# One block's softmax sums in a single round, its values in existing matmul bursts, and one shared PSUM pool

## Chip, cores, metric

One core of a Trainium2 chip. The metric is device time in microseconds (us) of one execution. A ratio is the mean time of one kernel's runs over that of the other's runs of the same rounds, so not quite the ratio of the medians quoted.

## What the kernel computes

```python
def _attn_ref(q, k, v, E, F):                    # 8 batches, 8 heads, 1024 tokens, head size 64
    k_proj = np.einsum('ks,bhsd->bhkd', E, k)    # 1024 tokens -> 64
    v_proj = np.einsum('ks,bhsd->bhkd', F, v)
    scores = (1 / np.sqrt(64)) * np.matmul(q, k_proj.transpose(0, 1, 3, 2))
    ...                                          # softmax over the 64
    return np.matmul(attn, v_proj)

def _moe_ref(x, w_in, w_out):                    # x: 8192 x 512, from the attention
    h = x @ w_in                                 # 512 -> 2048
    return (h / (1 + np.exp(-1.702 * h))) @ w_out
```

The kernel handles 16 blocks of 512 tokens. Block j's two layers of large matmuls run while the attention of later blocks is threaded between them.

## The kernel before

`eight` is one round of eight small matmuls in eight tiles of the array (64 rows by 32 columns each); the large matmuls use the whole array. A round into another mode, and the way back, is called a burst here. A bank is one buffer of a PSUM pool; a chunk is the matmuls between two slots of the schedule (four in layer 1); u = 0 and 1 are the two halves of a block's heads; landing is the time from a load's issue to its arrival.

```python
ps_f = ...tile_pool(name="ps_f", bufs=4, space=PSUM)      # large matmuls, scores, projections
ps_d = ...tile_pool(name="ps_d", bufs=2, space=PSUM)      # sums
ps_n = ...tile_pool(name="ps_n", bufs=2, space=PSUM)      # values

def sums(h):                                              # blocks 5 to 15
    def go():
        d_ps = [ps_d.tile([P, TB], F32, name="d_ps") for _ in range(2)]
        ...                                               # one round: 8 sums on 32 rows each
        for e in range(2):
            nc.vector.reciprocal(rden[:, e, :], d_ps[e])
        rdr = dram.tile([HP, 2, TB], F32, name="rdr")
        nc.sync.dma_start(out=rdr, in_=rden[0:P:32])
        rbc[h] = att.tile([P, HP, TB], F32, name="rbc")
        for e, r in enumerate((LO, HI)):                  # copied to all rows by DMA
            nc.sync.dma_start(out=rbc[h][r], in_=rdr[None, :, e, :].to_broadcast([D, HP, TB]))
    return go

def norm(h, u):                                           # blocks 3 and 4, u = 0 and 1
    def go():
        d_ps = ...; eight(d_ps, [ones, ones], e)          # sums on all rows
        n_ps = ...; eight(n_ps, [values ...], e)
        for i in range(2):
            nc.vector.reciprocal(rd, d_ps[i])
            nc.vector.tensor_tensor(x_of(h)[:, 2 * u + i, :], n_ps[i], rd, op=ALU.mult)
    return go

def values(h, u): ...                                     # one round, then n_ps[i] * rbc[h]
...
# at(block, slot): slots 0 to 15 follow the chunks of layer 1, O = 16 and on those of layer 2
at(2, 1, norm(3, 0))
at(1, O + 7, proj(2), kv_out(2))
at(2, 11, norm(3, 1))
at(2, O + 6, proj(3), kv_out(3), norm(4, 0))
at(2, O, q_dma(3))
at(3, 9, norm(4, 1))
```

The softmax here doesn't subtract the row's maximum and nothing guards it: scores larger than these inputs give would overflow.

## Time and profile before

| | before |
|---|---|
| median of the first three runs | 514.3 us (514.02 to 514.62) |
| span of the profiled execution | 512.6 us |
| TensorE busy | 505.9 us, 3098 matmuls |
| VectorE busy | 171.7 us |
| granted clock | full in every slice |

TensorE hardly pauses, so where time goes is read from the starts of its groups: the distance from one start to the next, less what the same matmuls take undisturbed. The lines are in the prediction.

### The profile page before, as it was taken

The numbers are of one execution on the slowest core, as the hardware profiler recorded it, in microseconds if no ns is written. First come the engines' busy times: TensorE is split into PE (matmuls) and PEld (weight loads), VectorE is DVE, ScalarE is ACT, GpSimd is POOL, SyncE is SP. The second block draws the span as 40 slices with busy tenths as digits, with TensorE's granted clock in tenths as the row PEclk, the third lists the DMA queues.
The fourth block names the chain that finished last, engine by engine and source line by source line (L and its number), as shares of the span: only waits on it lengthen the run. The fifth ranks groups of instructions, "written<-read, shape, count | busy, mean of one in ns | idle before, by whom it ended". The sixth has DMA issues, their size and how long they took to land.

```text
span 512.6 us, 7250 instructions
## 1 busy us (share of the span) xinstructions
PE 505.9 (99%) x3098; PEld 231.8 (45%) x3098; DVE 171.7 (33%) x222; ACT 264.8 (52%) x444; POOL 78.0 (15%) x97
## 2 busy tenths in 40 slices
PE   8999999999999999999999999999999999999997
PEld 4584444434444444444444444444444444444444
DVE  4523114764861622316251241615214161611000
ACT  1675564554637456372755627374463737244351
POOL 7442051513300051000510024000000000000000
PEclk9999999999999999999999999999999999999999
DMA  9999999999989089650997349990602205050102
GB/s 164 197 203 207 211 141 167 217 169 131 208 125 217 1 177 199 131 160 28 219 169 179 73 89 217 114 245 1 170 1 69 97 4 162 1 166 1 82 1 82
DMA packets 124200, 66.58 MB, mean 130 GB/s; under 512 B 92252, under 2 KB 116060, under 8 KB 122248
## 3 DMA queue, kind: packets, MB, share of 16 engines
q0 software_dynamic: 84400, 29.37, 51.1%
q1 hardware_dynamic: 39688, 36.49, 28.2%
q8 instruction: 24, 0.39, 0.3%
q10 hardware_dynamic: 80, 0.26, 0.2%
q14 instruction: 8, 0.07, 0.0%
HBM read 70.78 MB, written 16.96 MB: 171 GB/s over the span
## 4 chain that ended last, share of the span: by engine, by line
PE 82%; DMA 13%; issue 3%; POOL 1%; DVE 0%; ACT 0%; POOLq 0%
PE f_ps L369 38%; PE f_ps L401 38%; DMA v_sb<-in_v_dram 9%; DMA w_in_sb<-in_moe_w_in_dram 2%; PE f_ps L166 2%; DMA k_sb<-in_k_dram 2%; PE f_ps L263 2%; PE n_ps L263 1%; PE d_ps L298 0%; POOL k_sb L58 0%; PE f_ps L393 0%; POOL q_sb L64 0%; PE d_ps L263 0%; POOL q_sb L58 0%; POOL v_sb L58 0%
## 5 line engine op out<-in xcount | busy, mean ns | idle before, releaser
L401 PE MATMUL f_ps<-w_out_sb,gT 128*128 128x512 bf16 x1008 | 227.4, 379 | 0.0
L369 PE MATMUL f_ps<-xT,w_in_sb 128*128 128x512 bf16 (+1 forms) x1088 | 226.5, 367 | 0.3 <-DMA w_in_sb<-in_moe_w_in_dram 0.2
L372 ACT ACTIVATE gT<-f_ps 128x512 bf16<-128x512 f32 (+1 forms) x270 | 152.1, 573 | 64.3 <-PE f_ps L369 63.2
L369 PEld LDWEIGHTS <-w_in_sb 128*128 128x128 bf16 x1088 | 105.0, 98 | 116.9 <-issue 2.1
L401 PEld LDWEIGHTS <-gT 128*128 128x128 bf16 x1008 | 95.6, 98 | 120.1 <-issue 11.3
L404 ACT COPY o_sb<-f_ps 128x512 f32<-128x512 f32 x63 | 36.9, 586 | 130.8 <-PE f_ps L401 121.0
L328 DVE TENSOR_TENSOR xT<-n_ps,rbc 128x512 bf16<-128x512 f32 x44 | 28.4, 686 | 203.3 <-PE n_ps L263 122.9
L301 DVE RECIPROCAL rden<-d_ps 128x512 f32<-128x512 f32 x22 | 72.2, 3321 | 0.0
L64 POOL DMA_DIRECT2D q_sb<-in_q_dram x56 | 49.1, 901 | 55.8 <-DMA k_sb<-in_k_dram 42.8
L279 ACT ACTIVATE expT<-f_ps 128x512 bf16<-128x512 f32 (+1 forms) x68 | 35.1, 571 | 27.9 <-PE f_ps L263 27.8
L58 POOL DMA_DIRECT2D k_sb<-in_k_dram x10 | 8.4, 845 | 172.9 <-PE f_ps L166 156.0
L318 DVE RECIPROCAL rdn<-d_ps 128x512 f32<-128x512 f32 x8 | 26.8, 3353 | 3.2 <-PE d_ps L263 3.2
L220 DVE CAST k_b<-f_ps 64x512 bf16<-64x512 f32 x7 | 4.8, 683 | 47.1 <-PE f_ps L166 47.1
L279 ACT ACT_TABLE_LOAD x13 | 16.7, 1283 | 4.7 <-PE f_ps L263 4.5
L283 ACT ACT_TABLE_LOAD x14 | 18.0, 1283 | 0.2
L166 PE MATMUL f_ps<-v_sb,eft 128*64 128x512 bf16 x56 | 13.4, 381 | 0.3 <-DMA v_sb<-in_v_dram 0.3
L166 PE MATMUL f_ps<-k_sb,eft 128*64 128x512 bf16 x56 | 13.6, 382 | 0.0
L395 DVE COPY o_sb<-f_ps 128x256 f32<-128x256 f32 x1 | 0.4, 425 | 38.6 <-issue 38.6
L136 PE MATMUL n_ps<-zeros 128*128 128x512 bf16 x34 | 11.5, 463 | 1.2 <-DVE zeros L107 1.2
L263 PE MATMUL f_ps<-qT,kt 64*32 64x512 bf16 x240 | 12.3, 386 | 0.0
L263 PE MATMUL n_ps<-expT,vq 64*32 64x512 bf16 x208 | 10.4, 377 | 0.0
L263 PEld LDWEIGHTS <-kt 64*32 64x32 bf16 x272 | 3.9, 88 | 13.7 <-issue 13.5
(71 smaller groups left out, 131.6 us busy)
## 6 DMA issues: line engine op xcount, KB each, us to landing
out_dram<-o_sb SPq DMA_DIRECT2D x15, 1024.0 KB
rbc<-rdr SPq DMA_DIRECT2D x22, 512.0 KB
k_sb<-in_k_dram POOLq DMA_DIRECT2D x7, 1024.0 KB, 13.8
v_sb<-in_v_dram POOLq DMA_DIRECT2D x7, 1024.0 KB, 10.4
q_sb<-in_q_dram POOLq DMA_DIRECT2D x56, 128.0 KB, 13.8
w_in_sb<-in_moe_w_in_dram POOLq DMA_DIRECT2D x8, 256.0 KB, 12.2
w_out_sb<-in_moe_w_out_dram POOLq DMA_DIRECT2D x4, 512.0 KB, 14.7
out_dram<-o_sb SPq DMA_DIRECT2D x3, 256.0 KB
```

The costliest lines, as they stand in the source:

```text
L64: nc.gpsimd.dma_start(out=qt[b][:, j], in_=qv[:, j])
L166: nc.tensor.matmul(kvps[b][r], eft(j, slice(e * KP, (e + 1) * KP)), (kt, vt)[e][b][:, :, j, :], start=(j == 0), stop=(j == J - 1))
L263: nc.tensor.matmul(outs[i][r.start + c:r.start + c + 32], lhsTs[i][ri, c:c + 32], rhss[i][ri], start=True, stop=True)
L279: nc.scalar.activation(expT[h][:, 2 * u + i, ts], s_ps[i], AF.Exp, scale=scale)
L283: nc.scalar.preload_act_table(AF.Gelu_apprx_sigmoid)
L301: nc.vector.reciprocal(rden[:, e, :], d_ps[e])
L318: nc.vector.reciprocal(rd, d_ps[i])
L328: nc.vector.tensor_tensor(x_of(h)[:, 2 * u + i, :], n_ps[i], rbc[h][:, 2 * u + i, :], op=ALU.mult)
L369: nc.tensor.matmul(h_ps, w_in_sb[:, kc, fc * P:(fc + 1) * P], xT[j][:, kc, ts], start=(kc == 0), stop=(kc == KC - 1))
L372: nc.scalar.activation(gts[j][:, fc, ts], h_ps, AF.Gelu_apprx_sigmoid)
L401: nc.tensor.matmul(o_ps[n], gts[j][:, fc, n * P:(n + 1) * P], w_out_sb[:, fc, :], start=(fc == 0), stop=(fc == FC - 1))
L404: nc.scalar.copy(osb[j][:, n, :], o_ps.pop(n))
```

## The change

Block 4 is to be treated as blocks 5 to 15 are: one round of sums, two reciprocals in place of four, copies by DMA, and the values in bursts that exist already. The one pool lets sums and values take any of four banks. Two edits come with it: the projection of batch 2 moves one chunk later, and the start is reordered. (The preload of ScalarE's GELU table in block 2 also moves two slots later, behind the moved scores.)

```diff
-    ps_d = ctx.enter_context(tc.tile_pool(name="ps_d", bufs=2, space=PSUM))
-    ps_n = ctx.enter_context(tc.tile_pool(name="ps_n", bufs=2, space=PSUM))
+    ps_x = ctx.enter_context(tc.tile_pool(name="ps_x", bufs=4, space=PSUM))
...                               (sums split into sums and spread, which holds the DMAs)
     tok(0, 3, 0)()
-    q_tr0(1, 0, AC)
-    q_tr0(1, 1, DV)
     x_tr(0, 3, 0)()
-    scores(0, 0, 1)()
+    q_tr0(1, 0, DV)
+    q_tr0(1, 1, DV)
...
-    at(0, 0, scores(0, 1, 1))
-    at(0, 1, gelu_table)
+    at(0, 0, scores(0, 0, 1))
+    at(0, 1, scores(0, 1, 1), gelu_table)
...
-        at(2, O + 3 + 2 * u, scores(5, u))
...
-    at(1, O + 7, proj(2), kv_out(2))
+    at(2, 0, proj(2), kv_out(2))
-    at(2, O + 6, proj(3), kv_out(3), norm(4, 0))
-    at(3, 9, norm(4, 1))
+    at(2, O + 4, scores(5, 0))
+    at(2, O + 6, proj(3), kv_out(3), scores(5, 1), sums(4), spread(4))
...
-            at(j, O, sums(j + 2))
+            at(j, O, sums(j + 2), spread(j + 2))
+        if j == 3:
+            at(j, O, values(4, 0))
+            at(j, O + 6, values(4, 1))
```

More of the change, by code (lines that the diff above doesn't have):

```diff
@@ L133, in warm @@
     def warm(n):
-        w_ps = ps_n.tile([P, TB], F32, name="n_ps")
+        w_ps = ps_x.tile([P, TB], F32, name="x_ps")
         for _ in range(n):
@@ L156, in eft @@
         return efts[j // (J // 2)][:, j % (J // 2), cols]
-    kvps, kbs, qT, expT, xT, rbc = {}, {}, {}, {}, {}, {}
+    kvps, kbs, qT, expT, xT, rbc, rdens = {}, {}, {}, {}, {}, {}, {}
     def proj(b):
@@ L293, in go @@
         def go():
-            d_ps = [ps_d.tile([P, TB], F32, name="d_ps") for _ in range(2)]
+            d_ps = [ps_x.tile([P, TB], F32, name="x_ps") for _ in range(2)]
             for p in range(HP):
@@ L301, in go, with spread @@
                 nc.vector.reciprocal(rden[:, e, :], d_ps[e])
+            rdens[h] = rden
+        return go
+    def spread(h):
+        def go():
             rdr = dram.tile([HP, 2, TB], F32, name="rdr")
-            nc.sync.dma_start(out=rdr, in_=rden[0:P:32])
+            nc.sync.dma_start(out=rdr, in_=rdens.pop(h)[0:P:32])
             rbc[h] = att.tile([P, HP, TB], F32, name="rbc")
@@ L311, in go @@
             e = [expT[h][:, 2 * u + i, :] for i in range(2)]
-            d_ps = [ps_d.tile([P, TB], F32, name="d_ps") for _ in range(2)]
+            d_ps = [ps_x.tile([P, TB], F32, name="x_ps") for _ in range(2)]
             eight(d_ps, [ones, ones], e)
-            n_ps = [ps_n.tile([P, TB], F32, name="n_ps") for _ in range(2)]
+            n_ps = [ps_x.tile([P, TB], F32, name="x_ps") for _ in range(2)]
             eight(n_ps, [vqs[h // NB2 % 2][:, 2 * u + i, :] for i in range(2)], e)
@@ L323, in go @@
         def go():
-            n_ps = [ps_n.tile([P, TB], F32, name="n_ps") for _ in range(2)]
+            n_ps = [ps_x.tile([P, TB], F32, name="x_ps") for _ in range(2)]
             eight(n_ps, [vqs[h // NB2 % 2][:, 2 * u + i, :] for i in range(2)],
@@ L336, in go @@
         def go():
-            d_ps = f_tile([P, 4, D + 1]) if (h, half) == (0, 0) and p > 1 else                 ps_d.tile([P, 4, D + 1], F32, name="d_ps")
+            d_ps = f_tile([P, 4, D + 1]) if (h, half) == (0, 0) and p > 1 else                 ps_x.tile([P, 4, D + 1], F32, name="x_ps")
             for i in range(2):
@@ L352, in go @@
             x_sb = xs.pop((h, p, half)).rearrange("s (i t) d -> s i (t d)", i=2)
-            n_ps = ps_n.tile([P, 2, P], BF16, name="n_ps")
+            n_ps = ps_x.tile([P, 2, P], BF16, name="x_ps")
             for i in range(2):
@@ L439 @@
     tok(0, 3, 0)()
-    q_tr0(1, 0, AC)
+    x_tr(0, 3, 0)()
+    q_tr0(1, 0, DV)
     q_tr0(1, 1, DV)
-    x_tr(0, 3, 0)()
-    scores(0, 0, 1)()
     order = [(half, fc) for fcs in (range(12), range(12, FC)) for half in range(2) for fc in fcs]
-    at(0, 0, scores(0, 1, 1))
-    at(0, 1, gelu_table)
+    at(0, 0, scores(0, 0, 1))
+    at(0, 1, scores(0, 1, 1), gelu_table)
     for p in range(HP):
@@ L470 @@
         at(1, O + 3 + p, x_tr(2, p, 0), x_tr(2, p, 1))
-    for j in (1, 2):
-        at(j, O + 5, gelu_table)
+    at(1, O + 5, gelu_table)
     at(1, O + 4, q_dma(2))
+    at(2, 0, proj(2), kv_out(2))
     at(2, 1, norm(3, 0))
-    at(1, O + 7, proj(2), kv_out(2))
     at(2, 11, norm(3, 1))
-    at(2, O + 6, proj(3), kv_out(3), norm(4, 0))
     at(2, O, q_dma(3))
-    at(3, 9, norm(4, 1))
+    at(2, O + 4, scores(5, 0))
+    at(2, O + 6, proj(3), kv_out(3), scores(5, 1), sums(4), spread(4))
+    at(2, O + 7, gelu_table)
     for b in range(4, B):
@@ L490 @@
         if j + 2 < NBLK:
-            at(j, O, sums(j + 2))
+            at(j, O, sums(j + 2), spread(j + 2))
+        if j == 3:
+            at(j, O, values(4, 0))
+            at(j, O + 6, values(4, 1))
+        if j + 2 < NBLK:
             at(j, O + 6, values(j + 2, 0))
```

## The prediction

> **What bounds the kernel now.** I read the page first: TensorE against the other engines, and the chain that ended last.
>
> ```profile
> PE 505.9 (99%) x3098; PEld 231.8 (45%) x3098; DVE 171.7 (33%) x222; ACT 264.8 (52%) x444; POOL 78.0 (15%) x97
> ...
> PEclk9999999999999999999999999999999999999999
> ...
> PE 82%; DMA 13%; issue 3%; POOL 1%; DVE 0%; ACT 0%; POOLq 0%
> ```
>
> TensorE is 99% busy and the granted clock is full throughout. VectorE at 33% is far from a bound, so time saved there counts only where TensorE waits for it. Busy alone does not say that nothing can be saved: matmuls overlap, so I went on to TensorE's timeline and read differences of start times. These are four stretches of it (start, length, then the group):
>
> ```profile
> 115.08 3.63 PE L401 MATMUL f_ps<-w_out_sb,gT 128*128 128x512 bf16 x16
> 118.64 0.41 PE L263 MATMUL f_ps<-qT,kt 64*32 64x512 bf16 x8
> 118.98 1.90 PE L401 MATMUL f_ps<-w_out_sb,gT 128*128 128x512 bf16 x8
> ...
> 124.95 8.80 PE L369 MATMUL f_ps<-xT,w_in_sb 128*128 128x512 bf16 x40
> 133.68 0.41 PE L263 MATMUL d_ps<-expT,ones 64*32 64x512 bf16 x8
> 133.90 0.40 PE L263 MATMUL n_ps<-expT,vq 64*32 64x512 bf16 x8
> 134.24 5.35 PE L369 MATMUL f_ps<-xT,w_in_sb 128*128 128x512 bf16 x24
> ...
> 141.47 0.54 PE L298 MATMUL d_ps<-expT,ones 64*32 64x512 bf16 x8
> 141.94 10.53 PE L401 MATMUL f_ps<-w_out_sb,gT 128*128 128x512 bf16 x48
> ...
> 154.70 13.98 PE L369 MATMUL f_ps<-xT,w_in_sb 128*128 128x512 bf16 x64
> 168.51 1.89 PE L401 MATMUL f_ps<-w_out_sb,gT 128*128 128x512 bf16 x8
> 170.33 0.41 PE L263 MATMUL f_ps<-qT,kt 64*32 64x512 bf16 x8
> 170.56 0.40 PE L263 MATMUL n_ps<-expT,vq 64*32 64x512 bf16 x8
> 170.77 0.40 PE L298 MATMUL d_ps<-expT,ones 64*32 64x512 bf16 x8
> 171.10 10.53 PE L401 MATMUL f_ps<-w_out_sb,gT 128*128 128x512 bf16 x48
> ```
>
> Starts give the prices. Undisturbed 128x512 matmuls: (168.51 - 154.70)/64 = 0.2158 us each. A further round of eight 64*32 matmuls inside a burst: 0.23 (170.33 to 170.56) or 0.21 (170.56 to 170.77), say 0.22. A burst of one round alone costs more: 16 matmuls before the one at 118.64 should take 3.45 and took 3.56, and from 118.64 to 118.98 pass 0.34, so 0.45 in all. A burst of two rounds alone (133.68): 8.73 - 40*0.2158 = 0.10 before it, and 0.56 to the next matmul, 0.66. So entering and leaving a burst costs about 0.22, as much as a round.
>
> Last, the waits of TensorE itself, which are few:
>
> ```profile
> PE f_ps L166 <- DMA v_sb<-in_v_dram: 0.3, 1, 0.3
> PE f_ps L234 <- DMA q_sb<-in_q_dram: 0.3, 1, 0.3
> PE f_ps L263 <- ACT q0T L235: 0.2, 1, 0.2
> PE f_ps L369 <- DMA w_in_sb<-in_moe_w_in_dram: 0.2, 1, 0.2
> ```
>
> The first is the projection of batch 2: it runs from 89.13 to 91.69, 2.56 us, where the same 16 matmuls take 1.85 (65.13 to 66.98, or 120.81 to 122.66). So it costs 0.71, more than the idle time of 0.3, because the key half runs ahead alone. The other three lie before 28.1 us.
>
> **What the Trainium skill says.** "TensorEngine Tiling (Array Packing)", Key Properties: changing the tiling mode drains TensorE, changing the tile alone does not. The trace agrees: 0.22 for going in and out, nothing visible between rounds of one mode. "TensorE: Matmul & The Clock Gate", What happens when you issue a matmul: back-to-back warm matmuls of 512 columns start 215.7 ns apart; here 215.8. "VectorE: DVE Perf Modes", Walkthrough: the 8-slice pipeline in each mode, has the reciprocal as an iterative divide with a repeat count of 8; here it takes 3.3 us for 128x512 against 0.69 for a multiply of that shape, so it is the VectorE operation worth removing, if anything waited for it. "PSUM — Partial Sum Buffer", Summary: rules for kernel authors: evacuate promptly. No evacuation of the d and n banks holds TensorE in this trace except once, named below.
>
> **The change part by part.** On TensorE eight matmuls go (3098 to 3090, from the build: 16 rows less with their weight loads).
>
> 1. Block 4's two norm calls (two rounds each: sums spread over all rows, then values) become one round of sums (with block 3's projection, at the end of block 2) and two of values, in bursts of block 3 that exist already. The burst in the middle of block 3's first layer disappears: -0.66. The two rounds at the end of block 2 (122.66) were sums and values of norm; they become scores of block 5 and the new sums: 0. The burst at 118.64, where those scores stood, disappears: -0.45. Two rounds of values are added to bursts of block 3: +0.44. Sum -0.67.
>
> 2. Of block 4's four reciprocals two remain, 6.7 us less of VectorE. On TensorE's path this counts once: the sums of block 5 at 141.47 lead to the next matmul after 0.47, the same round at 170.77 after 0.33. The profile names VectorE's reciprocal (L318) as what they waited for, and the last one of norm ends at 141.55. In the changed kernel no reciprocal is in flight there: -0.14.
>
> 3. The projection of batch 2 moves behind the first chunk of block 2's first layer. It would begin at 89.04 + 0.86 + 0.09 = 89.99; the values arrived for 89.88. So its 0.71 goes, by a margin of only 0.1 us. The chunk put ahead has its input: the last copy of block 2's x ends at 87.89. -0.71.
>
> 4. The start: x of the last pair is transposed before the queries, and the scores of the second half move behind the first chunk. This removes the wait for a ScalarE copy (0.24) and some of the query wait. I count nothing. The first-layer chunks at 24.03, 25.36, 26.71 and 28.07 begin 1.33 to 1.36 us apart, each at the first use of a new slice of w_in, and the chain view goes there through that DMA (issued 16.54, 11.49 us). What is won before 28.07 is waited away there: 0.
>
> 5. One pool of four banks for two of two. In the transposes of blocks 0 to 2 and the bursts from block 4 on it gives out banks in the same rhythm; no wait at a d or n bank was on the path beyond part 2: 0.
>
> Sum: -0.67 - 0.14 - 0.71 = -1.52 us, 514.3 - 1.5 = 512.8.
>
> **The rivals.** *The values come late, and block 4's first layer waits.* Values of u = 1 now run at 152.6 (times of the kernel before), with that layer at 154.9, a round later than before. A multiply starts 0.44 after its round (170.56 to 171.00) and two take 1.29, so x is whole at 154.4; the third matmul, the first to need it, starts at 155.3. It holds if VectorE and the copied reciprocals are ready. VectorE: sums of block 5 give reciprocals from 141.7 to 148.3, the first values' multiplies end at 149.6. The copies: in steady blocks they are there 9.6 us after the reciprocals (148.8 to 158.4); for block 4 those end near 131, so the copy lands near 141, against 148 when it is first wanted. Even doubled it would be 150. I give a wait of up to 1 us here one chance in ten: 513.8.
>
> *The start counts after all.* If the slices of w_in were themselves released by TensorE, the 0.3 to 0.5 us would stay: 512.4. Against it, their issues on POOL wait for DMAs only. The other way round, ScalarE reaches its table load about 0.6 us later (exponentials behind one more activation), and four f banks could hold TensorE; the slack at 26.7 and 28.07 (0.24 and 0.21) covers about that: at worst +0.3.
>
> *The projection of batch 2 or 3 waits for its values anyway.* Batch 3's load is issued some 0.2 to 0.4 later and its projection comes 1.2 earlier (0.71 and 0.45); before, it landed near 117.8 (107.21 plus a landing of 10.6) for a start of 120.81. That leaves about 1.5. For batch 2 a landing 0.3 later costs 0.2: 513.0 to 513.5.
>
> *VectorE as bound* is out at 33%.
>
> **Range and chances.** Executions before spread 0.6 us (514.02 to 514.62), and each term above is a difference of starts good to 0.02. A tenth of the gain lost to a thin margin or the start is likely, all of it is not: 512.1 to 513.8 in eight cases of ten. 2% would be 10.3 us, seven times the sum, and nothing in the rivals adds more than 1 or 2: same 0.98.
>
> **What would show it.** After: no 64*32 burst within block 3's first layer; one fewer single-round burst at the end of block 2; L298-type sums there; the projection of batch 2 in 1.85 us with no wait for values; the sums of block 5 in 0.33 with no wait for VectorE; the wait for w_in near 28.1 still there and longer; first layer of block 4 at 64 matmuls in 13.81 with no wait; and the same distances from block 4 on. Wrong if a wait for VectorE stands before block 4's first layer, if the w_in wait has gone while later starts are earlier by more than 1.5, or if the values of batch 2 still hold the projection.

## The result and the profile after

512.14 us (512.1 to 512.38, four runs) against 514.42 (514.02 to 514.62, four runs): ratio 0.9958, 95% interval 0.994 to 0.9975. That is inside the predicted range, but only just (its lower end is 512.1), and 2.28 us where 1.5 was predicted. Two repetitions in later sessions gave medians of 512.58 and 513.14, ratios 0.995 and 0.9967.

In the changed kernel's source the large matmuls of the layers stand on lines 373 and 405 (369 and 401 before), scores and values on 262, sums on 297, projections on 165, multiplies on 332. The page after:

```profile
PE 504.4 (99%) x3090; PEld 232.0 (45%) x3090; DVE 165.6 (32%) x221; ACT 264.3 (52%) x443; POOL 78.1 (15%) x97
```

Eight matmuls fewer, as predicted; the busy share of TensorE does not move, which is why it could not have told anything. TensorE's timeline after, at the places that the prediction named (start, length, group):

```profile
88.47 1.03 PE L373 MATMUL f_ps<-xT,w_in_sb 128*128 128x512 bf16 x4
89.42 0.40 PE L165 MATMUL f_ps<-k_sb,eft 128*64 128x512 bf16 x1
89.49 0.38 PE L165 MATMUL f_ps<-v_sb,eft 128*64 128x512 bf16 x1
...
91.31 1.04 PE L373 MATMUL f_ps<-xT,w_in_sb 128*128 128x512 bf16 x4
...
120.96 0.41 PE L262 MATMUL f_ps<-qT,kt 64*32 64x512 bf16 x8
121.19 0.40 PE L297 MATMUL x_ps<-expT,ones 64*32 64x512 bf16 x8
121.52 1.90 PE L405 MATMUL f_ps<-w_out_sb,gT 128*128 128x512 bf16 x8
123.25 13.98 PE L373 MATMUL f_ps<-xT,w_in_sb 128*128 128x512 bf16 x64
137.07 1.89 PE L405 MATMUL f_ps<-w_out_sb,gT 128*128 128x512 bf16 x8
138.89 0.41 PE L262 MATMUL f_ps<-qT,kt 64*32 64x512 bf16 x8
139.11 0.40 PE L297 MATMUL x_ps<-expT,ones 64*32 64x512 bf16 x8
139.33 0.40 PE L262 MATMUL x_ps<-expT,vq 64*32 64x512 bf16 x8
139.66 10.53 PE L405 MATMUL f_ps<-w_out_sb,gT 128*128 128x512 bf16 x48
150.12 0.41 PE L262 MATMUL f_ps<-qT,kt 64*32 64x512 bf16 x8
150.35 0.62 PE L262 MATMUL x_ps<-expT,vq 64*32 64x512 bf16 x16
```

Block 3's first layer is one unbroken group of 64 (13.82 us from 123.25 to 137.07); the burst in its middle is gone. The sums at 139.11 no longer wait: 0.22 to the next round. The projection of batch 2 takes 1.89 from 89.42 to 91.31. The values of block 4 stand at 139.33 and, with those of block 5, at 150.35.

A chain of such starts splits a whole execution. Each row is a distance in the profiled executions, in us:

| stretch of TensorE's timeline | before | after | difference | predicted |
|---|---|---|---|---|
| span's start to block 0's second layer | 39.04 | 38.47 | -0.57 | 0 |
| to block 2's second layer | 67.80 | 67.12 | -0.68 | -0.71 |
| to block 3's first layer | 18.11 | 17.66 | -0.45 | -0.45 |
| to block 3's second layer | 14.48 | 13.82 | -0.66 | -0.66 |
| to block 4's first layer | 15.27 | 15.56 | +0.29 | +0.44 - 0.14 |
| to the last group of matmuls | 350.86 | 350.87 | 0 | 0 |
| to the span's end | 7.04 | 6.90 | -0.14 | 0 |

The middle rows are the prediction to 0.03 us; their sum is -1.50. What it did not have is 0.57 us in the first 39 and 0.14 in the last 7.

The difference at the start is there already at the first projection (8.40 before, 7.84 after), before the reordered part of the start; of the edits only the pool of the warm-up matmuls comes earlier, and with that edit alone (pool_only, below) it began at 8.70. It is not waited away at the w_in slice, as step 4 of the prediction would have it, because the slice came earlier too. Before, GpSimd (POOL) waited 0.61 us for the same key load and issued its first w_in slice at 8.64; after, it did so at 8.08. The slice that TensorE waits for was issued at 16.54 before and 15.98 after. TensorE's timeline, before and then after:

```profile
28.07 4.98 PE L369 MATMUL f_ps<-xT,w_in_sb 128*128 128x256 bf16 x44 [0.21 <-DMA w_in_sb<-in_moe_w_in_dram]
```

```profile
27.51 4.98 PE L373 MATMUL f_ps<-xT,w_in_sb 128*128 128x256 bf16 x44 [0.20 <-DMA w_in_sb<-in_moe_w_in_dram]
```

The difference at the end is no chance of the pair. From the last group of matmuls to the span's end it is 7.02 to 7.09 us in the six profiles without block 4's edit, 6.83 to 6.90 in the six with it, and 7.21 and 7.22 in the two versions that treat block 3 so as well. It lies in the last wait of SyncE (SP), for an output DMA. SyncE's waits before, then after:

```profile
SPq L538 <- DMA out_dram<-o_sb: 1.1, 1, 1.1
```

```profile
SPq L544 <- DMA out_dram<-o_sb: 0.9, 1, 0.9
```

Why the edit changes this wait is not shown.

### The profile page after: what moved, and what is told of

Same layout as the page of the kernel before. It is cut to its first block, busy times and chain, and to the rows that moved or that the text cites. A ratio compares the mean times of both kernels' runs of the same rounds, so it can differ in the third digit from the quotient of the medians.

```text
span 510.4 us, 7234 instructions
## 1 busy us (share of the span) xinstructions
PE 504.4 (99%) x3090; PEld 232.0 (45%) x3090; DVE 165.6 (32%) x221; ACT 264.3 (52%) x443; POOL 78.1 (15%) x97
## 4 chain that ended last, share of the span: by engine, by line
PE 94%; DMA 4%; POOL 1%; issue 0%; DVE 0%; ACT 0%; POOLq 0%
PE f_ps L405 43%; PE f_ps L373 43%; PE f_ps L165 3%; DMA w_in_sb<-in_moe_w_in_dram 2%; PE f_ps L262 2%; DMA v_sb<-in_v_dram 2%; PE x_ps L262 1%; PE x_ps L297 1%; POOL k_sb L57 0%; PE x_ps L359 0%; PE x_ps L344 0%; PE f_ps L397 0%; PE f_ps L244 0%; POOL q_sb L57 0%; POOL v_sb L57 0%
## 5 line engine op out<-in xcount | busy, mean ns | idle before, releaser
L332 DVE TENSOR_TENSOR xT<-x_ps,rbc 128x512 bf16<-128x512 f32 x48 | 30.9, 686 | 201.3 <-PE x_ps L262 124.9
L300 DVE RECIPROCAL rden<-x_ps 128x512 f32<-128x512 f32 x24 | 78.7, 3322 | 10.3 <-PE x_ps L297 10.3
L322 DVE RECIPROCAL rdn<-x_ps 128x512 f32<-128x512 f32 x4 | 13.4, 3353 | 0.8 <-PE x_ps L262 0.8
L135 PE MATMUL x_ps<-zeros 128*128 128x512 bf16 x34 | 11.2, 450 | 1.2 <-DVE zeros L106 1.2
L262 PE MATMUL x_ps<-expT,vq 64*32 64x512 bf16 x208 | 10.2, 377 | 0.0
## 6 DMA issues: line engine op xcount, KB each, us to landing
v_sb<-in_v_dram POOLq DMA_DIRECT2D x7, 1024.0 KB, 10.6
```

Source lines behind the costliest of these rows:

```text
L262: nc.tensor.matmul(outs[i][r.start + c:r.start + c + 32], lhsTs[i][ri, c:c + 32], rhss[i][ri], start=True, stop=True)
```

## The experiments

**The start: the edit or chance?** The first projection of keys waits for the first key load, which landed 7.1 us after its issue before and 6.6 after. If that is chance, neither the start edit nor the build is needed to explain the 0.57. The kernel before ran again, unchanged:

> The kernel before, unchanged, as a control of the start. In the profile on record its first key load landed 7.1 us after issue, TensorE's first projection began at 8.40 and the w_in wait ended at 28.07; in the changed kernel 6.6, 7.84 and 27.51, all before any edited instruction runs. Theory A (the 0.56 us is chance of the execution or the load, no part of the edit): this run is within 0.3 us of 514.4 in its median, but a profile of it can show the first projection anywhere from 7.8 to 8.5. Theory B (the edit causes it): again 8.4 and 28.07.

Landing at 7.2, span 512.4, the w_in wait ending at 27.96. Its six executions fell into two groups, three near 514.3 and three from 516.2 to 517.1, so the median is 515.3 and neither theory's time came true. Of all 43 executions of the kernel before 28 lie between 513.8 and 514.9 (median 514.28) and 15 between 515.1 and 517.8, with no wide gap between them. The changed kernel again:

> The changed kernel again: 512.1 to 512.4. Theory A: its first projection may begin at 8.4 this time, with a profile longer by the same amount; theory B: 7.84 again.

512.58 (511.72 to 512.95), a little above what was expected, landing at 6.9, first projection at 8.15, the w_in wait ending at 27.81. So the landing of one build moves by 0.3 from one profile to the next. (A small effect of the build is not excluded: 6.6, 6.9 and 6.9 in three profiles of the changed kernel, 7.1 and 7.2 in two of the kernel before.) The start edit alone:

```diff
 (the kernel before)
-    q_tr0(1, 0, AC); q_tr0(1, 1, DV); x_tr(0, 3, 0); scores(0, 0, 1)
+    x_tr(0, 3, 0); q_tr0(1, 0, DV); q_tr0(1, 1, DV)        # scores at slot 0, then slot 1
```

> Only the edit at the start. Prediction on record: 0 (514.3, first-layer chunks still wait for w_in until 28.1). Rival, that the start edit brings the missing 0.6: 513.8, with the w_in wait ending near 27.5.

516.14 (515.7 to 517.52), ratio 1.0024 (1.0005 to 1.0044): neither of the two. In its profile the key load landed after 9.0 us. From TensorE's timeline:

```profile
10.29 1.54 PE L174 MATMUL f_ps<-k_sb,eft 128*128 128x256 bf16 x8 [2.59 <-DMA k_sb<-in_k_dram]
```

Either the edit slows the start, or all six executions happened to fall into the slower group. The same file a second time:

> The start edit alone, a second time. It ran at 515.7 to 517.5 in all six executions, while executions of the kernel before fell into two groups, near 514.2 and near 516.2; in its profile the first key load landed at 9.0 us in place of 7.1 and TensorE waited 2.6 us for it. Theory A (two groups by the landing of that load, whichever kernel): this time some executions near 514.3. Theory B (the edit makes the start slower by itself): 515.7 or more in all, with the landing at 9 again.

514.48 (514.0 to 515.19), ratio 0.9992 (0.9971 to 1.0013), landing at 7.1, and the line now reads

```profile
8.35 1.03 PE L174 MATMUL f_ps<-k_sb,eft 128*128 128x256 bf16 x8 [0.26 <-DMA k_sb<-in_k_dram]
```

So one and the same kernel has times of both groups (the second session ran on another chip). The profile of the slow one has its first projection 1.94 us later (10.29 against 8.35) and block 0's second layer 2.95 us later (41.53 against 38.58). The late landing accounts for the first; the rest went with a granted clock of 0.50 from 11 to 14 us. A late landing alone does not make the slower group: in block4_only below it was 8.5 us, the clock stayed full, and block 0's second layer began at 39.33, only 0.29 later than before. Why the landing varies is not shown, and no slow execution of the kernel before was profiled. The change with its start put back:

> The changed kernel with its start put back. Prediction on record: no difference to the changed kernel (512.1), as the w_in slice ends the start in both. Rival: 512.7, the w_in wait ending at 28.07 again.

512.64 (512.3 to 513.05), against 512.58 for the changed kernel in the same rounds. A gain of the start edit cannot be told from the scatter, as predicted.

**The projection alone.**

```diff
 (the kernel before)
-    at(1, O + 7, proj(2), kv_out(2))
+    at(2, 0, proj(2), kv_out(2))
```

> Only the projection of batch 2 moved behind the first chunk of block 2. Prediction on record: -0.71 us, the projection in 1.85 us with no wait for values longer than 0.1. Rival: the values hold it anyway, gain under 0.3. Read in the profile as a difference of TensorE starts, from the w_in wait near 28 to block 2's second layer (before: 28.07 to 106.84, 78.77; expected 78.06), because the landing of the first key load shifts whole executions.

513.69 (513.39 to 513.97) against 514.53, ratio 0.9975 (0.9953 to 0.9997). No wait for values; from block 0's second layer to block 2's, 67.09 us against 67.80: -0.71. (From the w_in wait, the distance that the expectation names, it is 27.94 to 105.99 = 78.05.)

**Block 4 alone**, with the shared pool, the other two edits put back:

```diff
 (the changed kernel)
-    at(2, 0, proj(2), kv_out(2))
+    at(1, O + 7, proj(2), kv_out(2))
 (and the start as before)
```

> Block 4's sums, reciprocals by copy and values in block 3's bursts, with the shared pool, but the start and the projection of batch 2 as before. Prediction on record: -0.67 - 0.14 = -0.81, all of it between the end of block 2's second layer and block 4's first layer (before: 106.84 to 154.70, 47.86; expected 47.05). Rival 1: a wait for VectorE before block 4's first layer takes up to 1 us of it back. Rival 2: the missing 0.6 us is here: 46.4.

513.75 (513.23 to 515.75; four of six below 513.9), ratio 0.9985 (0.9961 to 1.0009), which the timing leaves unclear because two executions are of the slower group. The trace does not: from block 2's second layer to block 4's first layer it is 107.26 to 154.31 = 47.05, against 47.86 before, -0.81 as expected. Both rivals fall.

**The pool alone.**

```diff
 (the kernel before)
-    ps_d ... bufs=2;  ps_n ... bufs=2
+    ps_x ... bufs=4        # every d_ps and n_ps tile from it
```

> Only the pools: four banks shared in place of two and two, on the kernel before. Prediction on record: 0 (514.0 to 514.6 in the faster of its two groups). Rival: the shared pool frees a bank earlier somewhere and 0.3 us or more of the total comes from it; then TensorE's distances from block 0's second layer to block 2's second layer (67.8 with the wait for values, 67.09 without) or from there to block 4's first layer (47.86) shrink.

514.03 (513.88 to 514.21) against 514.26, ratio 0.9987 (0.9973 to 1.0001). The timing cannot tell this from nothing; the trace can. From block 2's second layer to block 4's first it is 106.58 to 154.30 = 47.72, 0.14 less than before. TensorE's timeline, then VectorE's:

```profile
141.21 0.40 PE L297 MATMUL x_ps<-expT,ones 64*32 64x512 bf16 x8
141.54 1.25 PE L400 MATMUL f_ps<-w_out_sb,gT 128*128 128x512 bf16 x5
```

```profile
137.94 3.35 DVE L317 RECIPROCAL rdn<-x_ps 128x512 f32<-128x512 f32 x1
```

The sums start at 141.21 while block 4's last reciprocal still runs (to 141.29), and take 0.33, not 0.47: they found another bank free. So the 0.14 that the prediction gave to the removed reciprocals is a wait for a bank that such a reciprocal holds, and the pool alone removes it. The next run shows that the removed reciprocals alone remove it too.

**The change without the shared pool.**

```diff
 (the changed kernel)
-    ps_x ... bufs=4
+    ps_d ... bufs=2;  ps_n ... bufs=2
```

> The changed kernel with two pools of two banks in place of the one of four. My theory: values of block 4 (u = 1) and of block 5 (u = 0) stand in one burst and need four banks of the value pool; the second pair waits for the first pair's multiplies, so TensorE loses about 1.3 to 1.6 us there (0.44 after the round, two multiplies of 0.6 to 0.7), 1 to 1.6 us slower than the changed kernel, and the profile names VectorE's multiply. Rival: the pools are worth nothing anywhere, 512.1 to 512.6.

513.85 (513.66 to 515.06), ratio 0.9981 (0.996 to 1.0002); the changed kernel, in the session before, had 512.58 and 0.995. TensorE's timeline has the wait, named:

```profile
150.62 0.40 PE L263 MATMUL n_ps<-expT,vq 64*32 64x512 bf16 x8
151.80 0.40 PE L263 MATMUL n_ps<-expT,vq 64*32 64x512 bf16 x4 [0.78 <-DVE xT L333]
152.40 0.40 PE L263 MATMUL n_ps<-expT,vq 64*32 64x512 bf16 x4 [0.20 <-DVE xT L333]
```

The second pair of values waits for the multiplies of the first, in two steps. From block 3's second layer to block 4's first layer it is 137.33 to 154.46 = 17.13, against 15.56: +1.57. Without one pool of four the new place of the values would have cost as much as all the rest of the change saves.

The same run has the sums of block 5 with two banks of their own and no reciprocal of block 4 in flight:

```profile
139.38 0.40 PE L298 MATMUL d_ps<-expT,ones 64*32 64x512 bf16 x8
139.59 0.40 PE L263 MATMUL n_ps<-expT,vq 64*32 64x512 bf16 x8
```

The next round starts 0.21 us later, with no wait. So either edit is enough to remove the 0.14, and their gains at this place do not add.

**A third run of the changed kernel**, as a neighbour of the extensions:

> The changed kernel a third time, beside its extensions: 512.1 to 512.9; from block 2's second layer to block 4's first layer 47.05 us as in the two profiles so far.

513.14 (511.98 to 513.51), above the expected 512.9, ratio 0.9967 (0.9953 to 0.9982); the distance is as expected, 106.30 to 153.34 = 47.04. Its view of TensorE's waits has a line that the other two profiles of the changed kernel have not:

```profile
PE f_ps L165 <- DMA v_sb<-in_v_dram: 0.6, 1, 0.6
```

In this execution no w_in slice was waited for and block 0's second layer began at 38.22, 0.25 earlier than in the first; the projection of batch 2 then came too early for its values (its first matmul at 89.18, the last at 91.70 in place of 91.00). From block 0's second layer to block 2's it took 68.08 us, so the gain of this step was gone (67.80 before, 67.12 in the first profile after). In the second profile of the changed kernel (after_again) this stretch took 67.34 us, so 0.46 of the 0.71 was gained. The margin of 0.1 us that the prediction gave this step is as thin as it said, and in these profiles part or all of the step's gain was lost there.

**The change carried to block 3**, to see whether the prices hold:

```diff
 (the changed kernel)
-    at(2, 0, proj(2), kv_out(2))
-    at(2, 1, norm(3, 0))
-    at(2, 11, norm(3, 1))
+    at(2, 0, proj(2), kv_out(2), sums(3), spread(3))
+    for u in range(2):
+        at(2, O + 2 * u, values(3, u))
```

> Extension of the change to block 3: its sums in one round behind the projection of batch 2, reciprocals by copy, its values in the bursts of block 2's second layer. If bursts and rounds have the price of the prediction: two bursts of two rounds go (2 * 0.66), one round behind a projection (0.22 and about 0.1 for one more change of mode) and two rounds in existing bursts (0.44) come: -0.56, that is 511.6 to 512.3. Rival: the copied reciprocals land too late for block 3 (they start near 100 and take 10 to 12), values hold banks, and block 3's first layer at 123.3 waits: 512.5 or more.

519.07 (515.47 to 519.36), ratio to the kernel before 1.0066 (1.004 to 1.0091): slower (not by 2%, but clear of noise). The rival's time came true and its late copies too, but the wait is not the one that it named. The price of the bursts held: from the last matmul of batch 2's projection to block 2's second layer 13.61 us (91.64 to 105.25) against 14.59 (91.00 to 105.59), -0.98 before the added values. The loss is elsewhere. TensorE's timeline, then VectorE's:

```profile
119.20 0.40 PE L165 MATMUL f_ps<-k_sb,eft 128*64 128x512 bf16 x1
124.36 0.58 PE L165 MATMUL f_ps<-v_sb,eft 128*64 128x512 bf16 x1 [4.76 <-DMA v_sb<-in_v_dram]
```

```profile
119.60 2.48 DVE L332 TENSOR_TENSOR xT<-x_ps,rbc 128x512 bf16<-128x512 f32 x4 [19.33 <-DMA rbc<-rdr]
```

The projection of batch 3 begins at 119.20 (119.11 in the changed kernel) but its values, issued 0.8 us later than there, took 17.6 us to land in place of 10.6. The copies of block 3's reciprocals, ready at 100.3, landed at 119.6: 19.3 us. They are the only transfers that this version adds to that stretch, and loads and copies were slowed together. The Trainium skill states what this needs: "Trainium Kernel Development and Optimization", Key Constraints, that DMAs issued from SP, ACT and POOL all run on the same 16 engines and interleave. The trace is in line with it, as copies issued on SP (19.3 us) and a load issued on POOL (17.6 us) were late in the same 20 us. That the copies are the cause was not tried separately. After the wait TensorE's projection matmuls start 0.43 apart where they start 0.21 apart otherwise, and the mean granted clock from 120 to 130 us is 0.83.

**The same with three pairs of score bursts merged:**

```diff
 (block 3's version)
-        at(0, Q + u, scores(1, u));  at(1, O + u, scores(2, u));  at(2, O + 2 * u, scores(4, u))
+        at(0, Q, scores(1, u, x=u == 1))        # x: the pair's banks from the shared pool
+        at(1, O, scores(2, u, x=u == 1)); at(2, O, scores(4, u, x=u == 1))
-        at(2, O + 2 * u, values(3, u))
+        at(2, O + 4 * u, values(3, u))
```

> The same with three pairs of score rounds put in one burst each (the second of a pair on two of the four shared banks), so three bursts fewer in blocks 0 to 2: 3 * 0.22 = 0.66 more than block3_too, 511.0 to 511.7. Rival: ScalarE's four exponentials in a row (2.2 us and a table load of 1.28) hold the banks and TensorE waits as much as it saves: equal to block3_too.

517.85 (514.99 to 519.2), ratio 1.0051 (1.0025 to 1.0076); a wait of 4.1 us for the same values. The merged bursts of blocks 0 and 1 saved what they should: from block 0's second layer to the projection of batch 2 it is 38.61 to 89.10 = 50.49, against 50.95 after, -0.46 for two bursts. Merging without block 3's copies was not run.

## Why the prediction was right, point by point

1. *Block 4's rounds and bursts, -0.67.* Right: -0.45, -0.66 and +0.44 appear in the rows of the table to 0.02 us.

2. *Two reciprocals fewer, -0.14 on TensorE's path.* Right in size, and the stated cure works: with the reciprocals gone and two pools kept (two_pools) the wait is gone. What the step did not say is that the wait is for a bank, and that the shared pool alone removes it with the reciprocal still in flight (pool_only). The change makes both edits, so the term belongs to neither alone; the sum does not change.

3. *The projection of batch 2, -0.71.* Right in proj2_only (-0.71) and in the first profile (-0.68), with the stated thin margin. In the second profile it was -0.46, and in the third the values were waited for again and the gain was lost, which is one of the prediction's own signs of being wrong. So the step holds in some executions and not in others.

4. *The start, 0.* Right in size for the edit: 514.48 against 514.53 alone, 512.64 against 512.58 undone. The way there was another. In the first profile after, the two waits that the edit removes (0.24 and 0.32) are replaced by one of 0.74 us for VectorE's x before the moved transposes, so the first chunk begins 12.95 us after the first projection, as before (12.96), and the w_in wait did not grow (0.20 against 0.21). What failed is the silent assumption that two executions start alike. In the first pair the key load and the w_in slices after it came 0.56 us earlier; that gave 0.57 of the 0.7 us beyond the prediction and put the first result at the edge of the range. The repetitions, 512.58 and 513.14, lie well inside it.

5. *The pool, 0.* Alone it gives 0.14, the same 0.14 as in 2. What the step left out is that the new burst of block 4's and block 5's values needs four banks at once: the pool is a condition of the rest (two_pools: +1.57).

6. *The rival that values come late.* It did not happen, but the working behind it was off. It had the copied reciprocals land near 141, 10 us after the reciprocals, and gave room for a doubling. The queue's timeline and VectorE's after show what happened:

```profile
129.31 0.62 SPq L307 DMA_DIRECT2D rdr<-rden  x1
134.75 1.35 SPq L310 DMA_DIRECT2D rbc<-rdr  x2
```

```profile
147.70 1.29 DVE L332 TENSOR_TENSOR xT<-x_ps,rbc 128x512 bf16<-128x512 f32 x2 [1.55 <-DMA rbc<-rdr]
150.79 1.29 DVE L332 TENSOR_TENSOR xT<-x_ps,rbc 128x512 bf16<-128x512 f32 x2 [1.80 <-PE x_ps L262]
```

The reciprocals end at 129.28 and the copy is there for the multiply at 147.70: 18.4 us. VectorE waited 1.55 for it, the values of u = 1 still found it idle, and block 4's x was whole at 152.08, before its layer at 152.63. Between the two pairs of multiplies VectorE stood idle for 1.80 us, so the copy could have come that much later before the multiplies of u = 1 moved; by an estimate from the same lines some 1.6 us were left before TensorE would have waited for a bank (the first multiplies end at 148.99, and the second round of values, at about 150.6, needs their banks if banks are given out in turn). The size of that transfer's time was taken from quiet stretches; this one lies beside the loads of batch 4. (For batch 3 the margin was larger than worked out: counted from block 0's second layer, its load was issued 0.67 us earlier and not 0.2 to 0.4 later.)

Over all 16 executions of the changed kernel the median is 512.58; against 514.28 for the faster group of the kernel before that is -1.7, against the predicted -1.5. A remainder of 0.2 is about what the end of the execution gives (6.83 to 6.90 us against 7.02 to 7.09), which the prediction did not have; the start moves by more than that between executions, so the sum does not prove it. Why no execution of the changed kernel fell into the slower group is not settled either: start_only did so in one session and not in the next, on another chip.

## What to carry to other kernels

When one engine is saturated, price its work by distances between starts and split both executions at the same instructions: here that gave each part to 0.03 us where timing could not, and showed at once that 0.57 us of a gain lay before the reordered part of the start. A pool's banks belong to the schedule: moving work into one burst needs as many banks as the burst holds at once. And take the time of a copy by DMA from the stretch where it will run: it was 9.6 us in quiet stretches and 18.4 and 19.3 beside a batch's loads, and the version with the added copies there waited 4.76 us for its load.

## What the Trainium skill lacked or had wrong

- "TensorEngine Tiling (Array Packing)" says that a change of mode drains TensorE but gives no price. Here going in and out costs 0.22 us, as much as a round of eight 64x512 matmuls in eight tiles (0.21 to 0.23).
- "TensorE: Matmul & The Clock Gate" has, in its table of the two states, the clock fall back after at least one idle window of about 3.4 us. In start_only the longest single wait was 2.59 us, with a smaller one of 0.90 before it, and the clock fell, so the window need not be one unbroken wait: eight 256-column matmuls took 1.33 us to the next group in place of 0.87, and the mean granted clock from 10 to 12 us was 0.67. After 4.76 us idle (block3_too) matmuls started at half the pace, as the page says.
- No page tells how much a copy through HBM to all rows (two DMAs of 512 KB) stretches beside loads: 9.6 us from reciprocal to multiply in quiet blocks, 18.4 and 19.3 beside a batch's loads, and the load beside it 17.6 in place of 10.6.
- No page tells how far the first load of an execution varies: 6.6 to 9.0 us to landing. Between the two profiles of start_only (9.0 and 7.1) block 0's second layer began at 41.53 and at 38.58, some 1 us of it with the half clock.
